# Folding a weight by halves, reading V in long rows that are transposed twice, and a second PSUM pair for attention values

## Chip, cores, metric

One core of one Trainium2 chip. The metric is the device time of one execution in microseconds (us); lower is better. All times compared below are of the state called fast; slow executions (over 1.5% above the fastest of the same kernel) are left out of the ratios, with one exception: run e12 has an execution of 313.05 us that is listed as slow, and its ratio comes out only with that execution counted in (see "The clock"). The quoted medians are over all executions.

## The reference

```python
def _attn_ref(q, k, v):                    # 8 batches, 8 heads, 576 rows, 64 columns
    scores = (1 / np.sqrt(64)) * np.matmul(q, k.transpose(0, 1, 3, 2))
    rel = pos[:, None] - pos[None, :]
    scores = np.where((rel >= 0) & (rel < 64), scores, -1e9)      # window of 64, causal
    attn = softmax(scores)
    return np.matmul(attn, v)

x = attn_out.transpose(0, 2, 1, 3).reshape(4608, 512)
out = ((x @ w1) * (x @ w2) @ w3) @ w_out   # w1, w2: 512x1024, w3: 1024x1024, w_out: 1024x512
```

## The kernel before

`w3 @ w_out` is folded once, on the chip, into `wc_sb`; after that, the feed-forward of a group of 512 rows is `ffn_ab` (eight times) and `ffn_o` (four times). Attention runs as `scores`, an exponential on ScalarE, masks on GpSimd, and `values`. The first two batches are a hand-ordered prologue; from the third on a loop interleaves attention of one batch with the feed-forward of another.

In these traces an engine takes its own instructions in program order. So where a line stands in this code decides what its copies stand behind. PSUM in the text is the memory that these kernels' matmuls write to (tiles f_ps, s_ps, o_ps and tp in the profile's lines) and that other engines then copy out of.

```python
def load_v(b, *blocks):                # V straight into key blocks, short rows, GpSimd queue
    ...
        nc.gpsimd.dma_start(out=vh[lo:P, c], in_=v[b, :, s0:s0 + P - lo, :].rearrange("h s d -> s h d"))
def copy_v(b, c):                      # rows that two key blocks share
    vh = v_heads(b)
    dve_cp(vh[0:D, c], vh[D:P, c - 1])
    if c == 1:
        dve_cp(vh[D:P, 1], vh[0:D, 2])
def fold_t(fc):                        # turn one block of w3
    ...
    dve_cp(w3T, tp)
def fold_mm(fc, w3T, cp):              # multiply it by the whole of w_out
    for ec in range(8):
        nc.tensor.matmul(o_ps, w3T[:, ec, :], wo16[:, ec, :], start=(ec == 0), stop=(ec == 7))
    cp(wc_sb[:, fc, :], o_ps)
def fold_step(fc):                     # the turn runs one block ahead of the fold
    if fc + 1 < 8:
        w3Ts[fc + 1] = fold_t(fc + 1)
    fold_mm(fc, w3Ts.pop(fc), act_cp if fc % 4 == 3 else dve_cp)
# ... cut: the prologue's first stretch
for d in range(5):
    ...
    values(d)
    if d < 4:
        scores(d + 2)
    fold_step(d + 2)
    # ... cut: loads of batch 1, its k casts on VectorE and ScalarE, its q casts on GpSimd and ScalarE
```

## Time and profile before

| | before |
|---|---|
| time, median of 3 (range) | 296.19 us (295.75 to 296.27) |
| profiled span | 294.3 us |
| first turn of w3 (the fold starts) | 19.71 us |
| first feed-forward matmul | 46.85 us |
| start of the repeating part | 81.27 us |

A timeline line gives start, length, engine, line of the kernel, operation, what it writes and reads, shapes, and in brackets the idle time just before with the engine or transfer that ended it. The readings of before, with their lines, are in the prediction. The stretches A (fold start to first feed-forward matmul), B (to the repeating part) and C (the rest) are used in the same sense throughout.

### The profile page before, as it was taken

Reading aid. Unit: us, or ns where it says so; the run is one execution under the profiler, and the core shown is the slowest. Engines: PE = TensorE matmul, PEld = TensorE weight load, DVE = VectorE, ACT = ScalarE, POOL = GpSimd, SP = SyncE. Lnnn points to the kernel's source line nnn. Section 1 sums busy time; section 2 is a strip of 40 time slices with the busy share of each in tenths; the row PEclk is TensorE's granted clock in tenths of the full one; section 3 lists DMA queues with packets and bytes.
Section 4 is the critical chain, followed back from the end, with each engine's and each line's share of the span. In section 5 each row is a group of like instructions: output and inputs, shape, how many; then the busy total and the mean of one; then the engine's idle time right before and its main releaser. Section 6 shows DMA issues by size and latency. Waiting matters only on the chain.

```text
span 294.3 us, 5925 instructions
## 1 busy us (share of the span) xinstructions
PE 274.1 (93%) x2254; PEld 152.9 (52%) x2254; DVE 185.4 (63%) x289; ACT 168.4 (57%) x281; POOL 180.8 (61%) x214
## 2 busy tenths in 40 slices
PE   7758889898799999999999999999999999999992
PEld 7544555444455555555555787555555445444440
DVE  0715688465787667687777866677867555554541
ACT  2513774676458647766686565487568866642300
POOL 8835995478749856696869463786595344402200
PEclk9999999999999999999999999999999999999998
DMA  6999999990277939094929470950094021012012
GB/s 231 219 181 201 265 278 212 373 131 36 74 266 264 72 110 321 39 85 143 322 20 100 136 295 2 155 73 1 20 171 40 0 74 72 0 38 109 0 57 95
DMA packets 51665, 38.85 MB, mean 132 GB/s; under 512 B 38784, under 2 KB 41856, under 8 KB 51632
## 3 DMA queue, kind: packets, MB, share of 16 engines
q0 software_dynamic: 41744, 9.96, 36.2%
q1 hardware_dynamic: 9888, 28.46, 26.6%
q8 instruction: 19, 0.31, 0.4%
q14 instruction: 14, 0.11, 0.1%
HBM read 38.80 MB, written 9.44 MB: 164 GB/s over the span
## 4 chain that ended last, share of the span: by engine, by line
PE 76%; DVE 6%; ACT 5%; DMA 4%; issue 3%; POOL 3%; POOLq 0%; DVEq 0%; ACTq 0%
PE f_ps L395 38%; PE f_ps L408 19%; PE o_ps L311 7%; PE tp L253 5%; DMA ab<-in_moe_w_dram 4%; PE s_ps L278 4%; DVE xT L327 2%; PE f_ps L454 2%; ACT ln_s L321 2%; ACT r L323 2%; POOL v L488 2%; DVE kT L257 1%; DVE xT L326 1%; ACT ln_s L320 1%; ACT pt L282 1%
## 5 line engine op out<-in xcount | busy, mean ns | idle before, releaser
L395 PE MATMUL f_ps<-xT,w_sb 128*128 128x512 f16 (+1 forms) x640 | 134.1, 358 | 0.0
L290 POOL TENSOR_SCALAR_AFFINE_SELECT pt<-pt 128x512 f16<-128x512 f16 (+1 forms) x64 | 52.1, 814 | 69.0 <-ACT pt L282 68.9
L395 PEld LDWEIGHTS <-w_sb 128*128 128x128 f16 x640 | 59.7, 98 | 50.7 <-issue 0.5
L408 PE MATMUL f_ps<-wc_sb,ab 128*128 128x512 f16 x288 | 67.1, 379 | 0.1
L401 DVE TENSOR_TENSOR ab<-f_ps,a_sb 128x512 f16<-128x512 f32 x72 | 49.8, 692 | 18.4 <-PE f_ps L395 15.8
L326 DVE TENSOR_TENSOR xT<-o_ps,r 64x384 f16<-64x384 f32 x48 | 26.4, 550 | 53.8 <-ACT r L323 53.6
L282 ACT ACTIVATE pt<-s_ps 128x1024 f16<-128x1024 f32 (+1 forms) x48 | 45.5, 949 | 18.0 <-PE s_ps L278 16.5
L400 ACT COPY a_sb<-f_ps 128x512 f32<-128x512 f32 x72 | 41.7, 579 | 24.8 <-PE f_ps L395 23.9
L292 POOL TENSOR_SCALAR_AFFINE_SELECT pt<-pt 128x512 f16<-128x512 f16 (+1 forms) x64 | 52.4, 819 | 4.4
L320 ACT ACTIVATE ln_s<-o_ps 64x384 f32<-64x384 f32 x48 | 23.4, 487 | 53.4 <-PE o_ps L311 53.3
L408 PEld LDWEIGHTS <-ab 128*128 128x128 f16 x288 | 26.9, 98 | 28.8 <-DVE ab L401 0.6
L233 POOL DMA_DIRECT2D v<-in_v_dram x40 | 33.9, 854 | 5.9 <-DMA ab<-in_moe_w_out_dram 4.1
L311 PE MATMUL o_ps<-pt,v 128*128 128x128 f16 (+1 forms) x384 | 27.9, 215 | 5.9 <-DVE xT L327 4.0
L311 PEld LDWEIGHTS <-v 128*128 128x128 f16 x384 | 23.5, 98 | 18.2 <-issue 3.5
L410 DVE COPY t2k<-f_ps 128x512 f32<-128x512 f32 x36 | 24.7, 690 | 11.6 <-PE f_ps L408 11.1
L327 DVE TENSOR_TENSOR xT<-o_ps,r 64x384 f16<-64x384 f32 x48 | 26.9, 561 | 0.6
L323 ACT ACTIVATE r<-ln_s 128x384 f32<-128x384 f32 x48 | 25.1, 523 | 1.5
L321 ACT ACTIVATE ln_s<-o_ps 64x384 f32<-64x384 f32 x48 | 23.1, 482 | 0.5
L278 PEld LDWEIGHTS <-kT 64*128 64x128 f16 x384 | 10.5, 94 | 16.5 <-issue 14.8
L278 PE MATMUL s_ps<-qT,kT 64*128 64x128 f16 (+1 forms) x384 | 18.2, 214 | 0.3 <-ACT pt L282 0.2
L257 DVE COPY kT<-tp 128x768 f16<-128x768 f16 x17 | 16.2, 952 | 0.1
L454 PE MATMUL f_ps<-ab,t2k 128*128 128x512 f16 x64 | 15.0, 379 | 0.4 <-DVE t2k L448 0.3
(59 smaller groups left out, 179.8 us busy)
## 6 DMA issues: line engine op xcount, KB each, us to landing
stage<-in_k_dram SPq DMA_DIRECT2D x16, 576.0 KB
stage<-in_q_dram SPq DMA_DIRECT2D x16, 576.0 KB
out_dram<-t2k SPq DMA_DIRECT2D x36, 256.0 KB
v<-in_v_dram POOLq DMA_DIRECT2D x32, 128.0 KB, 4.7
w_sb<-in_moe_w_dram POOLq DMA_DIRECT2D x4, 512.0 KB, 9.5
ab<-in_moe_w_out_dram POOLq DMA_DIRECT2D x1, 1024.0 KB, 10.6
ab<-in_moe_w_dram POOLq DMA_DIRECT2D x2, 512.0 KB, 12.6
xT<-in_moe_w_dram POOLq DMA_DIRECT2D x2, 512.0 KB, 16.2
```

The lines of the kernel that those rows point to most:

```text
L233: nc.gpsimd.dma_start(out=vh[lo:P, c], in_=v[b, :, s0:s0 + P - lo, :].rearrange("h s d -> s h d"))
L278: nc.tensor.matmul(s_ps[:, a, jj, c0:c0 + n], kT[half, j, k0:k0 + P], qT[half, j, q0:q0 + n], start=True, stop=True, skip_group_check=True)
L282: nc.scalar.activation(pt[:, :, :, 0:w], s_ps[:, :, :, 0:w], AF.Exp, bias=-SHIFT, scale=scale)
L290: nc.gpsimd.affine_select(out=sl, in_=sl, pattern=pat, compare_op=ALU.is_ge, fill=0.0, base=off, channel_multiplier=-1)
L292: nc.gpsimd.affine_select(out=sl, in_=sl, pattern=[[-s, m] for s, m in pat], compare_op=ALU.is_ge, fill=0.0, base=63 - off, channel_multip ...
L311: nc.tensor.matmul(o_ps[:, jj, o0:o0 + n], v16[:, si * 2 + bi, j0 + jj, a * D:a * D + P], pt[:, a, jj, c0:c0 + n], start=first, stop=(bi = ...
L323: nc.scalar.activation(r, y, AF.Exp, scale=-1.0)
L327: nc.vector.tensor_tensor(xs[D:P], o_ps[D:P, :, 192:384], r[D:P], ALU.mult)
L395: nc.tensor.matmul(d[:, f * n + c0:f * n + c1], w[:, dc, (fc + f) * P:(fc + f + 1) * P], xT[:, dc, xc:xc + c1 - c0], start=first, stop=(dc ...
L400: act_cp(a_sb[:, 0:nf * n], a_ps[:, 0:nf * n])
L401: nc.vector.tensor_tensor(ab[:, fc:fc + nf, lo:hi], b_ps[:, 0:nf * n].rearrange("p (f n) -> p f n", f=nf), a_sb[:, 0:nf * n].rearrange("p ...
L408: nc.tensor.matmul(o_ps, ab[:, fc, t * P:t * P + P], wc_sb[:, fc, :], start=(fc == 0), stop=(fc == 7))
```

## The change

Its intent: start the fold sooner by waiting for half of w_out; let the scores of batch 0 run before its V is there; read V of batches 0 and 1 with few large packets and put it in place by two rounds of transposes on TensorE; give the values two PSUM pairs in turn so that they need not wait for each other. w3 is turned in place. The core of the diff:

```diff
+    def load_rows(b, which):              # long rows, cast to fp16 by the transfer
+        t = sb.tile([P, 2, TI * D], FP16, name="rows")
+        for hh in range(2):
+            nc.gpsimd.dma_start(out=t[:, hh], in_=big_rows(which, b, hh))
+    def keys_of_v(b, js, into, cps):      # second transpose of V, into key blocks
+        for j, tp in zip(js, into):
+            for c in range(6):
+                nc.tensor.transpose(tp[:, c, :], turned["v", b][:, j, VBLK[c]:VBLK[c] + P], ident16)
+        ...
-        o_ps = ps_v.tile([P, 2, 512], FP32, name="o_ps")
+        o_ps = ps_v.tile([P, 2, 512], FP32, name="o_ps") if pool is None else \
+            ps_s.tile([P, 2, 512], FP32, name="s_ps")
-    def load_wo():
+    def load_wo(half):
-    def fold_mm(fc, w3T, cp):
+    def fold_mm(fc, half, cp, nf=1):
...
+    fold_t(0)
+    scores(2)
+    load_rows(1, "k")
+    fold_mm(0, 0, dve_cp)
+    fold_t(1)
+    scores(3)
+    fold_mm(1, 0, dve_cp)
...                                        # cut: the same for 2 and 3
+    cast_qk(0, "v", 0, dve_cp)
+    cast_qk(0, "v", 1, act_cp)
+    load_rows(1, "q")
+    transposes(0, "v", 0, 1, 2, into=spare(ps_v, "o_ps") + [tp_bank()], cps=[dve_cp, act_cp, dve_cp])
+    fold_t(4, act_cp)
+    fold_mm(4, 0, dve_cp)
+    keys_of_v(0, [0, 1, 2, 3], spare(ps_v, "o_ps") + spare(ps_s, "s_ps"), [dve_cp, act_cp, dve_cp, act_cp])
+    fold_t(5)
+    values(0)
+    fold_mm(5, 0, dve_cp)
+    fold_t(6)
+    values(1, ps_s)
+    fold_mm(6, 0, dve_cp)
...
+    for d in range(3, 6):
+        fold_mm(2 * d - 6, 1, dve_cp, 2)   # second half of w_out, two blocks at a time
+        values(d, ps_s if d % 2 else None)
+    fold_mm(6, 1, dve_cp, 2)
+    for hh in range(2):
+        cast_qk(1, "k", hh, dve_cp)
+    load_rows(1, "v")
+    for i in range(2):
+        load_w12(i, 1)
+    ffn_ab(0, 0)
+    transposes(1, "k", 0, 1, 2, into=spare(ps_s, "s_ps") + [tp_bank()])
+    ffn_ab(0, 1)
+    for hh in range(2):
+        cast_qk(1, "q", hh, dve_cp)
...
+    transposes(1, "q", 0, 1, 2, into=spare(ps_v, "o_ps") + [tp_bank()])
+    ffn_ab(0, 2)
+    scores(6)
+    cast_qk(1, "v", 0, dve_cp)
+    cast_qk(1, "v", 1, act_cp)
+    transposes(1, "v", 0, 1, 2, into=spare(ps_v, "o_ps") + [tp_bank()], cps=[dve_cp, act_cp, dve_cp])
```

More of the change, by code (lines that the diff above doesn't have):

```diff
@@ L195, with big_rows @@
     v16s = [const.tile([P, 6, NJ, 4 * D], FP16, name=f"v16_{i}") for i in range(2)]
-    raws, k16s, q16s = {}, {}, {}
+    raws, t16s = {}, {}
+    def big_rows(which, b, hh):
+        return {"k": k, "q": q, "v": v}[which][b, hh:H:2].rearrange("j (p r) d -> p j (r d)", r=TI)
     def load_qk(b, which, gate=None):
-        src = k if which == "k" else q
-        t = sb.tile([P, 2, TI * D], FP32, name="stage", bufs=4)
+        t = sb.tile([P, 2, TI * D], FP32, name="stage", bufs=3)
         if gate is not None:
@@ L205, in load_qk, with t16_of @@
         for hh in range(2):
-            nc.sync.dma_start(out=t[:, hh], in_=src[b, hh:H:2].rearrange("j (p r) d -> p j (r d)", r=TI))
+            nc.sync.dma_start(out=t[:, hh], in_=big_rows(which, b, hh))
         raws[which, b] = t
-    def cast_qk(b, which, hh, cp):
-        t = raws[which, b]
-        if hh == 0:
-            (k16s if which == "k" else q16s)[b] = sb.tile([P, TI, P], FP16, name=which + "16", bufs=1)
-        t16 = (k16s if which == "k" else q16s)[b]
-        cp(t16[:, :, hh * D:hh * D + D], t[:, hh].rearrange("p (i d) -> p i d", d=D))
-    def cast_third(b, which, c, cp):
-        t = raws[which, b]
-        if c == 0:
-            (k16s if which == "k" else q16s)[b] = sb.tile([P, TI, P], FP16, name=which + "16", bufs=1)
-        t16 = (k16s if which == "k" else q16s)[b]
-        cp(t16[:, 6 * c:6 * c + 6].rearrange("p i (hh d) -> p hh i d", hh=2),
-           t[:, :, 6 * c * D:6 * c * D + 6 * D].rearrange("p hh (i d) -> p hh i d", d=D))
+    def load_rows(b, which):
+        t = sb.tile([P, 2, TI * D], FP16, name="rows")
+        for hh in range(2):
+            nc.gpsimd.dma_start(out=t[:, hh], in_=big_rows(which, b, hh))
+        raws[which, b] = t
+    def t16_of(b, which):
+        if (which, b) not in t16s:
+            t16s[which, b] = sb.tile([P, TI, P], FP16, name=which.replace("v", "k") + "16", bufs=1)
+        return t16s[which, b]
+    def cast_qk(b, which, hh, cp):
+        cp(t16_of(b, which)[:, :, hh * D:hh * D + D], raws[which, b][:, hh].rearrange("p (i d) -> p i d", d=D))
+    def cast_third(b, which, c, cp):
+        cp(t16_of(b, which)[:, 6 * c:6 * c + 6].rearrange("p i (hh d) -> p hh i d", hh=2),
+           raws[which, b][:, :, 6 * c * D:6 * c * D + 6 * D].rearrange("p hh (i d) -> p hh i d", d=D))
     def v_heads(b):
@@ L239, in copy_v @@
             dve_cp(vh[D:P, 1], vh[0:D, 2])
-    kTs, qTs = {}, {}
+    turned = {}
     def transposes(b, which, *cs, into=None, cps=None):
-        t16, dst = (k16s, kTs) if which == "k" else (q16s, qTs)
+        t16 = t16s[which, b]
         if cs[0] == 0:
-            dst[b] = sb.tile([P, NJ, S], FP16, name=which + "T")
+            turned[which, b] = sb.tile([P, NJ, S], FP16, name=which + "T", bufs=1 if which == "v" else 2)
+        dst = turned[which, b]
         if into is None:
@@ L252, in transposes @@
             for i in range(6):
-                nc.tensor.transpose(tp[:, i, :], t16[b][:, 6 * c + i, :], ident16)
+                nc.tensor.transpose(tp[:, i, :], t16[:, 6 * c + i, :], ident16)
         if cps is None:
@@ L256, in transposes @@
         for c, tp, cp in zip(cs, into, cps):
-            cp(dst[b].rearrange("q j (p i) -> q j p i", i=TI)[:, :, :, 6 * c:6 * c + 6],
+            cp(dst.rearrange("q j (p i) -> q j p i", i=TI)[:, :, :, 6 * c:6 * c + 6],
                tp.rearrange("q i (p j) -> q j p i", p=TP))
+    def keys_of_v(b, js, into, cps):
+        for j, tp in zip(js, into):
+            for c in range(6):
+                nc.tensor.transpose(tp[:, c, :], turned["v", b][:, j, VBLK[c]:VBLK[c] + P], ident16)
+        for j, tp, cp in zip(js, into, cps):
+            cp(v16s[b % 2][:, :, j].rearrange("p c (a e) -> p c a e", a=2)[:, :, :, 0:D],
+               tp.rearrange("p c (a e) -> p c a e", a=2))
     MASKS = [[(0, 1, 128, 0, 0), (128, 1, 64, 64, 0)]] + 2 * [[(0, 2, 128, 64, -64)]]
@@ L267, in scores @@
         si, jp = divmod(r, 2)
-        kT, qT = kTs[b], qTs[b]
+        kT, qT = turned["k", b], turned["q", b]
         seg = SEGS[si]
@@ L280, in scores @@
                 c0 += n
-        pt = sb.tile([P, 2, 2, 256], FP16, name="pt", bufs=3)
+        pt = sb.tile([P, 2, 2, 256], FP16, name="pt", bufs=6)
         nc.scalar.activation(pt[:, :, :, 0:w], s_ps[:, :, :, 0:w], AF.Exp, bias=-SHIFT, scale=scale)
@@ L294, in scores, with values @@
         probs[d] = pt
-    def values(d):
+    def values(d, pool=None):
         b, r = divmod(d, 6)
@@ L430, in load_w12 @@
                             in_=(moe_w1, moe_w2)[i][:, cols].rearrange("(c p) n -> p c n", p=P))
-    def load_wo():
-        nc.gpsimd.dma_start(out=wo16, in_=moe_w_out.rearrange("(e p) m -> p e m", p=P))
+    def load_wo(half):
+        cols = slice(half * 256, half * 256 + 256)
+        nc.gpsimd.dma_start(out=wo16[:, :, cols], in_=moe_w_out[:, cols].rearrange("(e p) m -> p e m", p=P))
     def load_w3(n):
@@ L439, in load_w3, with turned_w3, fold_t @@
         nc.gpsimd.dma_start(out=dst, in_=moe_w3[fc * P:fc * P + 2 * P].rearrange("(f p) n -> p f n", p=P))
-    def fold_t(fc):
-        w3 = w3_rows(fc).rearrange("p a (e n) -> p (a e) n", n=P)
+    def turned_w3(fc):
+        return w3_rows(fc).rearrange("p a (e n) -> p (a e) n", n=P)
+    def fold_t(fc, cp=dve_cp):
+        w3 = turned_w3(fc)
         tp = ps_f.tile([P, 8, P], FP16, name="f_ps")
@@ L446, in fold_t @@
             nc.tensor.transpose(tp[:, ec, :], w3[:, ec, :], ident16)
-        w3T = sb.tile([P, 8, P], FP16, name="t2k", bufs=4)
-        dve_cp(w3T, tp)
-        return w3T
-    def fold_mm(fc, w3T, cp):
-        o_ps = ps_f.tile([P, DM], FP32, name="f_ps")
-        for ec in range(8):
-            nc.tensor.matmul(o_ps, w3T[:, ec, :], wo16[:, ec, :], start=(ec == 0), stop=(ec == 7))
-        cp(wc_sb[:, fc, :], o_ps)
+        cp(w3, tp)
+    def fold_mm(fc, half, cp, nf=1):
+        cols = slice(half * 256, half * 256 + 256)
+        o_ps = ps_f.tile([P, 2, 256], FP32, name="f_ps")
+        for f in range(nf):
+            for ec in range(8):
+                nc.tensor.matmul(o_ps[:, f], turned_w3(fc + f)[:, ec, :], wo16[:, ec, cols],
+                                 start=(ec == 0), stop=(ec == 7), skip_group_check=True)
+        cp(wc_sb[:, fc:fc + nf, cols], o_ps[:, 0:nf])
     rows = 2 * 3 * B
@@ L491 @@
     ones_of(1)
-    load_wo()
+    load_wo(0)
     load_w3(0)
-    load_v(0, 0, 2, 3)
-    for n in range(1, 4):
-        load_w3(n)
-    load_v(0, 4, 5)
-    w3Ts = {}
-    def fold_step(fc):
-        if fc + 1 < 8:
-            w3Ts[fc + 1] = fold_t(fc + 1)
-        fold_mm(fc, w3Ts.pop(fc), act_cp if fc % 4 == 3 else dve_cp)
+    load_w3(1)
+    load_rows(0, "v")
+    load_w3(2)
+    load_w3(3)
+    load_wo(1)
     def spare(pool, name):
@@ L509, in spare, with tp_bank @@
         return [t[:, i, 0:768].rearrange("p (i n) -> p i n", i=6) for i in range(2)]
+    def tp_bank():
+        return ps_t.tile([P, 6, P], FP16, name="tp")
     keep_busy(75)
@@ L518 @@
         cast_third(0, "q", c, act_cp if c == 1 else dve_cp)
-    tps = [tps[3], ps_t.tile([P, 6, P], FP16, name="tp"), spare(ps_s, "s_ps")[0]]
-    transposes(0, "q", 0, 1, 2, into=tps, cps=[act_cp, dve_cp, act_cp])
+    transposes(0, "q", 0, 1, 2, into=[tps[3], tp_bank(), spare(ps_s, "s_ps")[0]], cps=[act_cp, dve_cp, act_cp])
     keep_busy(15)
     scores(0)
-    keep_busy(10)
+    keep_busy(12)
     scores(1)
-    keep_busy(30)
     for i in range(2):
         load_w12(i, 0)
-    w3Ts[0] = fold_t(0)
@@ L529 @@
-    fold_step(0)
-    fold_mm(1, w3Ts.pop(1), dve_cp)
-    copy_v(0, 1)
-    for d in range(5):
-        if d == 0:
-            w3Ts[2] = fold_t(2)
-        values(d)
-        if d < 4:
-            scores(d + 2)
-        fold_step(d + 2)
-        if d == 0:
-            load_v(1, 0, 2)
-            load_qk(1, "k", nc.vector.memset)
-            load_qk(1, "q")
-        if d == 1:
-            load_v(1, 3)
-        if d == 2:
-            copy_v(0, 4)
-            for i in range(2):
-                load_w12(i, 1)
-        if d == 3:
-            load_v(1, 4)
-            cast_qk(1, "k", 0, dve_cp)
@@ L552 @@
-    cast_qk(1, "k", 1, act_cp)
-    cast_qk(1, "q", 0, pool_cp)
-    cast_qk(1, "q", 1, act_cp)
-    values(5)
-    fold_step(7)
-    transposes(1, "k", 0, 1, into=spare(ps_s, "s_ps"))
-    transposes(1, "k", 2)
+    keep_busy(12)
+    fold_t(0)
[5 more added lines that the diff above has]
+    fold_mm(1, 0, dve_cp)
+    fold_t(2)
+    scores(4)
+    fold_mm(2, 0, act_cp)
+    fold_t(3)
+    scores(5)
+    fold_mm(3, 0, dve_cp)
+    cast_qk(0, "v", 0, dve_cp)
@@ new lines @@
+    cast_qk(0, "v", 1, act_cp)
[10 more added lines that the diff above has]
+    fold_mm(6, 0, dve_cp)
+    fold_t(7)
+    values(2)
+    fold_mm(7, 0, dve_cp)
+    for d in range(3, 6):
+        fold_mm(2 * d - 6, 1, dve_cp, 2)
+        values(d, ps_s if d % 2 else None)
@@ L559 @@
+    fold_mm(6, 1, dve_cp, 2)
[4 more added lines that the diff above has]
+        load_w12(i, 1)
     for n in range(3):
         keep_sums(n)
-    load_v(1, 5)
+    ffn_ab(0, 0)
[3 more added lines that the diff above has]
+        cast_qk(1, "q", hh, dve_cp)
     load_qk(2, "k", nc.gpsimd.memset)
     load_qk(2, "q")
-    load_v(2, 0, 2, 3)
-    ffn_ab(0, 0)
@@ L566 @@
-    transposes(1, "q", 0, 1, into=spare(ps_s, "s_ps"))
-    transposes(1, "q", 2)
-    copy_v(1, 1)
-    ffn_ab(0, 1)
+    transposes(1, "q", 0, 1, 2, into=spare(ps_v, "o_ps") + [tp_bank()])
     ffn_ab(0, 2)
     scores(6)
+    cast_qk(1, "v", 0, dve_cp)
+    cast_qk(1, "v", 1, act_cp)
+    load_v(2, 0, 2, 3)
+    transposes(1, "v", 0, 1, 2, into=spare(ps_v, "o_ps") + [tp_bank()], cps=[dve_cp, act_cp, dve_cp])
     ffn_ab(0, 3)
     scores(7)
-    steps = [lambda fc=fc: ffn_ab(0, fc) for fc in range(4, 8)] + [lambda t=t: ffn_o(0, t) for t in range(3)]
@@ L577 @@
-    for d in range(6, 11):
-        values(d)
-        if d < 10:
-            scores(d + 2)
-        for _ in range(2 if d in (6, 8) else 1):
-            steps.pop(0)()
-            store()
+    keys_of_v(1, [0, 1, 2], spare(ps_v, "o_ps") + [tp_bank()], [dve_cp, act_cp, dve_cp])
+    scores(8)
+    keys_of_v(1, [3], [tp_bank()], [dve_cp])
+    steps = [lambda fc=fc: ffn_ab(0, fc) for fc in range(4, 8)] + [lambda t=t: ffn_o(0, t) for t in range(4)]
+    for d in range(6, 12):
+        values(d, ps_s if d in (9, 11) else None)
+        if d < 9:
+            scores(d + 3)
+        steps.pop(0)()
+        store()
@@ L584 @@
         if d == 6:
             load_v(2, 4, 5)
-            copy_v(1, 4)
             load_qk(3, "k")
-        else:
-            which, hh = [("k", 0), ("k", 1), ("q", 0), ("q", 1)][d - 7]
-            cast_qk(2, which, hh, pool_cp)
-    transposes(2, "k", 0, 1, into=spare(ps_s, "s_ps"))
-    values(11)
+        if d < 10:
+            cast_qk(2, "kq"[(d - 6) // 2], d % 2, pool_cp)
+    transposes(2, "k", 0, 1, into=spare(ps_v, "o_ps"))
     transposes(2, "k", 2)
@@ L595 @@
         cast_qk(3, "k", hh, pool_cp)
-    ffn_o(0, 3)
+    steps.pop(0)()
     store()
@@ L599 @@
     transposes(2, "q", 2)
+    load_qk(3, "q")
+    steps.pop(0)()
+    store()
     copy_v(2, 1)
     copy_v(2, 4)
-    load_qk(3, "q")
     for n in range(3, 6):
```

## The prediction

> **What bounds the kernel now.** I first read the busy shares by slice on the profile's page: the TensorE row is at 9 from the eleventh of 40 slices to the last but one, and uneven before that.
>
> ```profile
> PE   7758889898799999999999999999999999999992
> DMA  6999999990277939094929470950094021012012
> ```
>
> So what is open to a gain lies in the first quarter. The chain of work that ended last gave me where to cut it: the weight fold starts at 19.71 us, when the first rows of w3 land; the feed-forward starts at 46.85; and at 81.27 the prologue is over and the repeating part begins, whose code the diff does not touch. A table of busy time in these three stretches (length, then TensorE matmul, weight load, VectorE, ScalarE, GpSimd, then clock, DMA share, GB/s):
>
> ```profile
> 19.71:46.85 27.14, 24.09 (x227) 13.86 (x228) 17.59 (x31) 15.87 (x26) 23.59 (x30) 1.00 1.39 237
> 46.85:81.27 34.42, 30.14 (x249) 16.02 (x247) 22.75 (x36) 19.28 (x33) 22.50 (x26) 1.00 0.77 160
> 81.27:294.30 213.03, 206.67 (x1594) 111.06 (x1590) 139.37 (x217) 126.35 (x214) 121.43 (x142) 0.99 0.47 106
> ```
>
> TensorE is idle 27.14 - 24.09 = 3.1 us in the first stretch (call it A), 4.3 us in the second (B). In C it is 97% busy, so whatever moves the start of C moves the end. The waits themselves, from the timeline of TensorE alone (start, length, what, and in brackets idle time before and who ended it):
>
> ```profile
> 19.71 1.07 PE L446 MATMUL f_ps<-ident,ab 128*128 128x128 f16 x16 [2.71 <-DMA ab<-in_moe_w_dram]
> ...
> 36.58 0.61 PE L311 MATMUL o_ps<-pt,v 128*128 128x128 f16 x8 [0.27 <-DVE xT L327]
> 37.12 0.40 PE L278 MATMUL s_ps<-qT,kT 64*128 64x128 f16 x8
> 37.45 0.62 PE L446 MATMUL f_ps<-ident,xT 128*128 128x128 f16 x8
> 37.91 1.89 PE L454 MATMUL f_ps<-ab,t2k 128*128 128x512 f16 x8
> 39.97 0.62 PE L311 MATMUL o_ps<-pt,v 128*128 128x128 f16 x8 [0.18 <-DVE xT L327]
> ```
>
> One round of A (values, scores, turn of w3, fold) lasts 3.4 us. The chain of o (two logarithms of 0.49, a reciprocal of 0.53, two multiplications of 0.56 us, then the next values) lasts just as long, so the single PSUM pair for o costs only 0.2 to 0.3 us a round. The lines by shape give the unit costs (count, busy us, mean ns of one, idle before):
>
> ```profile
> L257 DVE COPY kT<-tp 128x768 f16<-128x768 f16 x17 | 16.2, 952 | 0.1
> L257 ACT COPY qT<-tp 128x768 f16<-128x768 f16 x5 | 4.0, 808 | 0.0
> L448 DVE COPY t2k<-f_ps 128x1024 f16<-128x1024 f16 x8 | 5.4, 691 | 7.9 <-PE f_ps L446 7.7
> L214 ACT CAST k<-stage 128x1152 f16<-128x1152 f32 x1 | 1.1, 1136 | 0.0
> L214 DVE CAST k<-stage 128x1152 f16<-128x1152 f32 x1 | 0.8, 845 | 0.0
> ```
>
> [...]the 32 matmuls that cross the ring's end (two cuts for 512 columns, so 256 on average) took 3.49 us, 109 ns each, against 3.45 us for 16 of 512. So halves cost TensorE nothing. [...]here 768 fp16 elements out of PSUM take 0.95 us and 512 within SBUF (the V copies) 0.29. [...]in the windows of 1 us the casting queue writes 200 to 210 GB/s with weights alone and 155 to 160 while V blocks are among them. [...]the loss is small.
>
> **The change part by part.**
>
> *Start of the fold.* Before it 1.05 MB of w_out and 0.52 MB of w3 have to land (written bytes). Half of w_out is now enough: 0.52 MB less at 200 GB/s is 2.6 us; with the V blocks no longer close behind, 3.3. The 12 dummy matmuls left after the second scores end near 16.0, so the fold starts at about 16.4: 3.3 us gained. V, the rest of w3, the other half and w1, w2 land by about 36 at 205 GB/s, ahead of their use.
>
> *Work added to TensorE.* Each of two batches gets 18 + 24 transposes for V. Six in a stream move the chain by 0.34 us[...], so 84 cost 4.8 us. Nothing is removed from it but 16 dummy matmuls that only filled a wait.
>
> *The upper limit.* 3.3 earlier + 3.1 + 4.3 of idle time, less 4.8 of new work: 5.9 us, if no wait were left. That is just 2%.
>
> *Waits in A, set down engine by engine in program order from the fold's start (0).* A round of scores, turn and half fold is 0.45 + 0.33 + 0.86 of TensorE, but fold follows the turn of the same rows: turn, copy 0.69, then fold, and the copy also stands behind the last fold's eviction (about 0.38). Such a round is 2.3 us with 0.6 idle; four end at 9.1. The casts of V stand behind the last eviction on VectorE and the last exp on ScalarE, so V's first transposes start at 10.4 (1.3 idle) and end at 11.4. Fold 4 waits for ScalarE's copy of 1024 columns until 13.1; the second transposes end at 15.4, their copies at 16.5. Values 0, 1, 2 go in at 16.0, 18.5, 21.7: the copy of each turn stands behind the multiplications of the values before on VectorE, so the folds wait 0.7 to 1.4 us each. Then the four double folds and three values run dense until 31.9, and the feed-forward waits for the last multiplication: 33.0. Of these 33 us TensorE works 23.8. A thus ends at 16.4 + 33 = 49.4, against 46.85, and the 18 transposes of k, which stood in A, are still to come.
>
> *Waits in B, from its start (0).* Casts and copies that GpSimd and ScalarE shared are on VectorE. Transposes of q wait for two casts (about 0.6 each, fp16 source; an estimate from 0.29 for 512 elements) that stand behind three 0.95 copies of k and one product: start 7.5, TensorE idle since 4.7, 2.8 us. Transposes of V wait for a cast on ScalarE of 1.1 behind the exp: 2.2 us. The fourth group of V's second transposes waits for its PSUM bank to be copied: 1.1. Values 7 and 8 wait for o, 0.8 each, as now; smaller ones sum to some 2.5. TensorE's work is 28.4 (now, by starts) + 1.0 (k) + 2.4 (V) = 31.8; with about 10 of waits, 42. VectorE has some 34 us of work in it, against 22.75. C starts at 49.4 + 42 = 91.4, against 81.3.
>
> The sum is +10 us. I don't take it whole: a worked list counts every wait in full, and a wait of 0.3 to 0.5 put wrong in each of twenty places is 6 to 10 us, more likely too much than too little, since I rounded starts upward. I take some 70%: +7, so 303.
>
> **The rivals.** *The earlier fold wins through:* the copies and casts fall into gaps, the two PSUM pairs remove the waits for o, and C starts 1 to 4 us earlier: 292 to 295. For it: VectorE is busy only 65% in A and 66% in B, and all its new work there is under the length. Against it: [...]the new copies stand between turn and fold. *DMA is the true limit:* shares above 1 in A and V's 36,864 small packets of 41,744 suggest a gain through A and B from long rows. Against it: TensorE's only long wait for DMA is the 2.7 us at the start; V's 9,216 packets less free nothing on the path. It would give 291 to 294. *A new transfer wait:* rows of V of batch 1 and the second halves of w1 and w2 are now issued on GpSimd only after a cast at the end of A, so they land near 60, needed at 61 and 69; two us late would add two: 305 to 308. *The repeating part suffers* from three input buffers in place of four; by the order of loads and casts each slot is free before it is wanted, so nothing.
>
> **Range and chances.** 303, range 293.5 to 309.5: the low end is the first rival, the high end the full sum and a late transfer. Faster by over 2% needs more than the limit above: 3%. Within 2% (up to 302.1) holds the first two rivals and the lower part of my sum: 39%. Slower: 58%.
>
> **What would show it.** Right: fold's first turn near 16.4; first feed-forward matmul near 49; waits of TensorE before the folds for VectorE's copies of the turned w3, and before the transposes of q and V for casts; start of C near 88 to 91; C as long as now, 213. Wrong: C starting before 82, or the fold's rounds below 2.0 us, or C shorter by 3 us or more, which no step here explains.

## The result

The changed kernel took 309.97 us (median of four, 308.72 to 311.48) against 296.18 (median of four): ratio 1.047, 95% interval 1.042 to 1.052. Ratios in this text are the mean time of one kernel's fast runs over that of the other's fast runs of the same rounds, so not quite the ratio of the quoted medians; those of the experiments come out, as far as they can be redone from the listed times, only if the profiled execution is left out. The kernel got slower, as held likeliest, but by 13.8 us where 6.8 was predicted, and just outside the range.

The table by stretch of the kernel after; columns as in the prediction (length, TensorE matmul, weight load, VectorE, ScalarE, GpSimd, then clock, DMA share, GB/s):

```profile
16.18:50.51 34.33, 26.86 (x314) 23.43 (x315) 18.92 (x32) 17.77 (x28) 15.32 (x21) 0.95 0.77 135
50.51:95.61 45.10, 36.81 (x309) 20.63 (x307) 29.84 (x46) 22.55 (x37) 26.28 (x32) 0.92 0.70 146
95.61:308.20 212.59, 206.65 (x1591) 111.03 (x1589) 138.90 (x216) 125.83 (x214) 121.47 (x142) 1.00 0.48 107
```

The fold starts 3.5 us earlier (16.18 against 19.71). A is 7.2 us longer, B 10.7 us longer, C the same within 0.5 us. The repeating part starts at 95.61 instead of 81.27: 14.3 us later, which is the whole loss. The third column from the right is the one whose change the prediction had no step for: the mean granted TensorE clock is 0.95 in A and 0.92 in B, where it was 1.00 in both before.

The waits of TensorE in A and B, longest groups first (what it was about to do, what it waited for: sum, times, longest), kernel after:

```profile
PE f_ps L477 <- DVE xT L469: 2.3, 3, 1.8
PE o_ps L261 <- DVE q L225: 2.1, 1, 2.1
PE f_ps L477 <- ACT xT L469: 2.0, 1, 2.0
PE o_ps L261 <- ACT k L225: 2.0, 1, 2.0
PE f_ps L477 <- DVE ab L469: 1.8, 4, 0.5
PE o_ps L329 <- DVE xT L345: 1.3, 2, 0.7
```

L477 is the fold, L469 the copy of the turned w3, L261 the transposes of q, k and V, L225 a cast (V uses the name of k). So these are the waits that the prediction set down: folds for the copy that they follow at once, transposes for their casts. On TensorE's timeline, with what came after each (kernel after):

```profile
16.18 0.62 PE L468 MATMUL f_ps<-ident,ab 128*128 128x128 f16 x8 [0.23 <-DMA ab<-in_moe_w_dram]
...
30.39 1.05 PE L477 MATMUL f_ps<-ab,xT 128*128 128x256 f16 x8 [2.02 <-ACT xT L469]
...
54.31 1.89 PE L413 MATMUL f_ps<-xT,w_sb 128*128 128x512 f16 x8
...
58.26 0.93 PE L261 MATMUL o_ps<-ident,q 128*128 128x128 f16 x12 [2.05 <-DVE q L225]
...
59.61 3.22 PE L413 MATMUL f_ps<-xT,w_sb 128*128 128x512 f16 x8
...
65.12 0.95 PE L261 MATMUL o_ps<-ident,k 128*128 128x128 f16 x12 [2.01 <-ACT k L225]
...
66.50 3.19 PE L413 MATMUL f_ps<-xT,w_sb 128*128 128x512 f16 x8
```

The group of eight feed-forward matmuls at 54.31 takes 1.89 us, as before. The same group takes 3.22 us shortly after the wait at 58.26 and 3.19 us after the one at 65.12. Windows of one microsecond show the reason, the third number from the right being the granted clock:

```profile
32.00:33.00 1.00, 1.00 (x12) 1.00 (x10) 0.50 (x1) 0.00 (x0) 0.00 (x0) 0.50 1.27 219
60.00:61.00 1.00, 1.00 (x4) 0.41 (x3) 1.00 (x2) 0.79 (x1) 0.00 (x0) 0.50 1.20 260
```

After each of the three waits of 2.0 us the clock is at half for 3.4 us (a dip, below): 0.50, where it is 1.00 around it. The dips start at 31.58, 58.88 and 65.71 us (by windows of 0.1 us), and each lasts 3.41 us. The second and third start 8.0 and 10.0 times 3.41 us after the first, so in this trace they lie on a grid of 3.41 us; a step of the grid, counted from a dip of the same run, is called a window in what follows. The windows just before the three dips hold 2.02, 2.05 and 2.01 us of idle TensorE time. The length of a wait alone does not tell what follows it: after the wait of 2.71 us in the kernel before the clock is 1.00.

In the two runs set side by side here it goes with where in a window a wait falls. The profiled execution of e12 (below; only the issue of two transfers is moved) has the same three waits, of 2.02, 2.05 and 2.01 us, and a single dip, from which its windows are counted back. Two windows of the kernel after, the one with the wait before q's transposes and the next, then the windows of e12 with its second wait (two windows) and its third, and the next (TensorE's busy time is the second number):

```profile
55.47:58.88 3.41, 1.36 (x15) 0.75 (x14) 2.73 (x5) 0.49 (x1) 0.73 (x2) 1.00 1.00 180
58.88:62.30 3.42, 3.42 (x17) 1.77 (x15) 1.82 (x2) 1.40 (x2) 0.00 (x0) 0.50 1.17 265
```

```profile
53.14:56.55 3.41, 2.07 (x15) 0.87 (x12) 3.36 (x5) 0.59 (x1) 0.60 (x2) 1.00 0.79 121
56.55:59.97 3.42, 2.70 (x26) 1.70 (x26) 2.48 (x4) 0.83 (x2) 0.00 (x0) 1.00 1.03 323
59.97:63.38 3.41, 1.40 (x26) 1.13 (x26) 1.10 (x3) 2.31 (x3) 1.81 (x4) 1.00 1.03 416
63.38:66.79 3.41, 3.41 (x13) 1.23 (x10) 1.78 (x2) 1.40 (x2) 2.86 (x4) 0.50 1.19 373
```

The wait of 2.05 us is cut in two by the end of a window (1.34 and 0.72 us idle), and the clock stays at 1.00; the one of 2.01 us lies inside a window, and the next is at 0.50. No clean limit comes out of the runs, though. In e12 a fourth wait, of 2.20 us up to 38.03, lies with 1.95 us in one window by the same count, and the folds after it take their usual 1.05 us. In e1 (below) the window from 37.86 to 41.27, counted on from its dip at 27.62, has 2.03 us idle, and the groups after it are as fast as ever (0.61 and 1.05 us). In e11, against that, two waits of 0.96 and 0.72 us between 57.7 and 60.3 us are followed by a group of 3.23 us in place of 1.90. So idle time within a window is not all that counts, and what else does was not shown. The number of dips may then differ between executions of one kernel, and the times fit that: e12's four executions take 307.30, 308.69, 311.39 and 313.05 us at mean clocks of 0.989, 0.984, 0.973 and 0.967.

Last, the GpSimd queue. It stood for 21.55 us before the DMA issue of the rows of V of batch 1, which waited for a cast on VectorE, with the second halves of w1 and w2 behind them, and the transfer engines were almost idle from 38 to 54 us (the DMA row has one digit per 7.7 us slice; digits six and seven fall there):

```profile
53.53 1.07 POOL L216 DMA_DIRECT2D rows<-in_v_dram  x2 [21.55 <-DVE k L225]
```

```profile
DMA  6999900999416993829483954092049003003012
```

### The profile page after: what moved, and what is told of

Read it like the earlier page. It is cut to its first block, busy times and chain, and to the rows that moved or that the text cites. A ratio compares the mean times of both kernels' runs of the same rounds, so it can differ in the third digit from the quotient of the medians.

```text
span 308.2 us, 6193 instructions
## 1 busy us (share of the span) xinstructions
PE 282.2 (92%) x2386; PEld 165.9 (54%) x2386; DVE 193.1 (63%) x300; ACT 173.1 (56%) x286; POOL 176.1 (57%) x212
## 4 chain that ended last, share of the span: by engine, by line
PE 76%; DVE 9%; ACT 5%; DMA 4%; issue 2%; POOL 2%; POOLq 0%; ACTq 0%; DVEq 0%
PE f_ps L413 36%; PE f_ps L426 20%; PE o_ps L329 5%; PE tp L261 5%; PE s_ps L295 4%; PE f_ps L477 3%; DMA ab<-in_moe_w_dram 3%; POOL v L512 2%; DVE xT L345 2%; DVE kT L265 2%; DMA stage<-in_k_dram 1%; ACT ln_s L339 1%; ACT r L341 1%; DVE xT L344 1%; ACT pt L299 1%
## 5 line engine op out<-in xcount | busy, mean ns | idle before, releaser
L413 PE MATMUL f_ps<-xT,w_sb 128*128 128x512 f16 (+1 forms) x640 | 137.1, 363 | 0.6 <-DVE xT L345 0.6
L413 PEld LDWEIGHTS <-w_sb 128*128 128x128 f16 x640 | 60.6, 99 | 53.0 <-issue 4.5
L344 DVE TENSOR_TENSOR xT<-o_ps,r 64x384 f16<-64x384 f32 x43 | 23.6, 550 | 47.3 <-ACT r L341 47.3
L338 ACT ACTIVATE ln_s<-o_ps 64x384 f32<-64x384 f32 x43 | 20.9, 487 | 36.8 <-PE o_ps L329 36.1
L329 PE MATMUL o_ps<-pt,v 128*128 128x128 f16 x344 | 24.9, 216 | 1.7 <-DVE xT L345 1.7
L240 POOL DMA_DIRECT2D v<-in_v_dram x30 | 25.4, 854 | 0.0
L345 DVE TENSOR_TENSOR xT<-o_ps,r 64x384 f16<-64x384 f32 x43 | 24.1, 561 | 0.6
L339 ACT ACTIVATE ln_s<-o_ps 64x384 f32<-64x384 f32 x43 | 20.7, 482 | 0.5
L225 POOL CAST k<-stage 128x1152 f16<-128x1152 f32 x12 | 13.8, 1151 | 2.0 <-PE tp L261 2.0
```

What stands on the lines that cost most here:

```text
L329: nc.tensor.matmul(o_ps[:, jj, o0:o0 + n], v16[:, si * 2 + bi, j0 + jj, a * D:a * D + P], pt[:, a, jj, c0:c0 + n], start=first, stop=(bi = ...
L344: nc.vector.tensor_tensor(xs[0:D], o_ps[0:D, :, 0:192], r[0:D], ALU.mult)
L345: nc.vector.tensor_tensor(xs[D:P], o_ps[D:P, :, 192:384], r[D:P], ALU.mult)
L413: nc.tensor.matmul(d[:, f * n + c0:f * n + c1], w[:, dc, (fc + f) * P:(fc + f + 1) * P], xT[:, dc, xc:xc + c1 - c0], start=first, stop=(dc ...
```

## The experiments

Theory: the loss is the sum of waits that the new program order makes (turn directly before its fold; casts before transposes), in full and not at 70%, plus lost clock after the longest. Rivals: the transfers issued late are the limit; or one part alone (the transposes of V) carries the loss. The runs undo parts of the change, or fill waits without removing them.

| run | what was altered | ratio to before (95%) |
|---|---|---|
| the change | | 1.047 (1.042 to 1.052) |
| e1_fill_waits | three waits filled with dummies | 1.042 (1.039 to 1.044) |
| e8_fill_all | five waits filled | 1.040 (1.036 to 1.044) |
| e9_fill_all_w12_early | five filled, w1 and w2 issued sooner | 1.033 (1.030 to 1.036) |
| e12_w12_early | only w1 and w2 issued sooner | 1.048 (1.043 to 1.054) |
| e2_q_cast_gpsimd | q casts off VectorE | 1.034 (1.029 to 1.040) |
| e3_turn_ahead | turn one block ahead of fold | 1.025 (1.021 to 1.029) |
| e4_v_blocks | V as before | 1.025 (1.020 to 1.030) |
| e6_one_pair | one PSUM pair for the values | 1.062 (1.058 to 1.066) |
| e7_whole_w_out | whole w_out first | 1.053 (1.045 to 1.061) |
| e5_three_undone | e2, e3 and e4 | 1.009 (1.006 to 1.012) |
| e10_three_undone_w12_early | e5, w1 and w2 sooner | 1.008 (1.003 to 1.012) |
| e11_rebuilt | all rewritten, halves and pairs kept | 1.012 (1.007 to 1.016) |
| e13_order_of_before | e10 up to the feed-forward, then before's code | 0.999 (0.995 to 1.003) |
| e14_v_copy_scalar | e13, three copies of V on ScalarE | 0.993 (0.990 to 0.996) |
| e15_v1_before_q_cast | e14, first V blocks of batch 1 sooner | 0.991 (0.987 to 0.995) |

All outputs are right. The line numbers of the experiments' profiles differ by a few from those of the kernel after.

### The clock

The change's own profile has three dips. e1 puts 28 dummy matmuls, some 1.7 us, into each of three waits; nothing can start sooner for it.

```diff
     fold_t(4, act_cp)
+    fill(28)
     fold_mm(4, 0, dve_cp)
...
+    fill(28)
     transposes(1, "q", ...
...
+    fill(28)
     transposes(1, "v", ...
```

> 28 dummy matmuls (1.7 us at 0.062 each) are put into three waits of TensorE of 2.0 us each (before the fold of rows 4, before the transposes of q and of V of batch 1). In the changed kernel the granted clock falls to 0.50 for some 3.3 us after each of these waits. Theory (part of the loss is the clock): no stretch at 0.50 is left between 28 and 70 us, the feed-forward group at 59.6 takes 1.9 us in place of 3.2 and the one at 66.5 too, the repeating part starts 3 to 4.5 us earlier, 305.5 to 307 us. Rival (the waits alone, the clock is made good elsewhere): within 1 us of 310.

Measured: 308.91 us, 1.6 less than after in the ratio's terms (0.0054 of 296); the profiled execution, 306.87, is the fastest of the four and alone inside the expected range. The timeline of TensorE in e1:

```profile
56.91 1.73 PE L509 MATMUL f_ps<-ident 128*128 128x128 f16 x28
59.12 0.84 PE L261 MATMUL o_ps<-ident,q 128*128 128x128 f16 x12 [0.49 <-DVE q L225]
59.80 0.50 PE L261 MATMUL tp<-ident,q 128*128 128x128 f16 x6
60.14 1.89 PE L413 MATMUL f_ps<-xT,w_sb 128*128 128x512 f16 x8
```

TensorE gets to its transposes no sooner after the group before them than without dummies, but the group after them is back at 1.89 us from 3.22. So here idle TensorE time, not the work itself, brought the half clock. The time fell by less than expected: the dip at 31 to 35 us was only replaced by one at 27.6 to 31.0 (0.50 in windows of one microsecond), after a wait of 1.68 us that I had not filled, and a wait of 0.5 us for w1 or w2 appeared. e8 fills two more waits.

```diff
+    fill(18)
     transposes(0, "v", ...
...
+    fill(24)
     fold_mm(6, 0, dve_cp)
```

> As the first filler run, and also 18 dummies before the transposes of V of batch 0 (wait 1.3 us) and 24 before the fold of rows 6 (wait 1.8 to 2.2). Theory (the granted clock is part of the loss): no stretch under 0.9 of the full clock between 20 and 75 us, 2.5 to 4.5 us less than the changed kernel, 305.5 to 307.5, and less spread from run to run. Rival (a low clock costs nothing, since TensorE waits anyway): 308.5 to 310.

Measured 309.15 us (2.2 below after by the ratio): a miss. The list of TensorE's waits in e8 starts with:

```profile
PE f_ps L413 <- DMA w_sb<-in_moe_w_dram: 2.9, 1, 2.9
```

TensorE is now at a point where the late halves of w1 and w2 are needed, and waits for them 2.9 us; the four matmuls behind that wait (74.15) take 1.89 us where the four before it took 1.04, and the next two groups are slow as well (0.85 for 0.51, 0.61 for 0.40), until 77.15: the half clock again, as an estimate from these lengths. e9 issues them earlier, ahead of the rows of V that hold up the queue; e12 does this alone.

```diff
     load_rows(1, "q")
+    for i in range(2):
+        load_w12(i, 1)
...
-    for i in range(2):
-        load_w12(i, 1)
```

> As the run with all waits filled, and the second halves of w1 and w2 are issued on GpSimd before the rows of V of batch 1 (which wait there for the casts of k) and not behind them. Theory (filling the waits gained only 1 us because the feed-forward then ran into these weights, a wait of 2.9 us on DMA, which the changed kernel hid behind its own lateness): that wait goes, 305.5 to 307.5. Rival (the clock is worth no more than 1 us): 308.5 to 310.

> The changed kernel with only the earlier issue of the second halves of w1 and w2, a control. Theory (there the weights land some 4 us ahead of use, since TensorE is late): 309 to 311, no change. Rival (the issue order itself costs the changed kernel time): under 308.

Measured: e9 306.69 us, e12 310.04. Both as expected. e12's ratio of 1.048 counts the slow execution of 313.05 us; without it 310.04 us, or 1.045, is left (from two executions, so a rough figure). e9 is then 3.6 us below its control e12 by the ratio, 3.3 by medians, and 4.3 below the change itself by the ratios of the table. Windows of 4 us show a clock of 1.00 throughout from 20 to 92 us in e9. The late transfer is not on the path of the changed kernel (e12 does not differ from it within the noise) but is the next limit behind the clock (e8). The lost clock is worth 3.3 to 4.3 us.

### The program order

e3 lets each turn run one block ahead. It also casts V one fold earlier and moves the copy of the fifth turn from ScalarE to VectorE (not shown):

```diff
     fold_t(0)
     scores(2)
-    fold_mm(0, 0, dve_cp)
     fold_t(1)
+    fold_mm(0, 0, dve_cp)
     scores(3)
-    fold_mm(1, 0, dve_cp)
     fold_t(2)
+    fold_mm(1, 0, dve_cp)
...
```

> The turn of each w3 block stands one block ahead of its fold, as in the kernel before; all else as changed. Theory: the four waits of 0.46, the 2.0 before the fold of rows 4, and the 1.8, 0.3 and 0.2 further on go (6.2 us in all), and the low clock after the second one (about 1.6 us); some of it comes back as waits for the casts of V: 4 to 7 us less, 303 to 306. Rival (w3's arrival or the logarithms of o bound this stretch): under 2 us less.

Measured 304.32 us: 6.6 us by the ratio. The feed-forward starts at 45.51 instead of 50.51. The four waits of the folds for VectorE's copy, 1.8 us in all, and the one of 2.0 us for ScalarE's are gone from the list. The three edits were not separated.

e2 moves the q casts of batch 1 from VectorE, behind three copies of 0.95 us, to GpSimd, right after `fold_mm(7, 0, ...)`:

```diff
     fold_mm(7, 0, dve_cp)
+    for hh in range(2):
+        cast_qk(1, "q", hh, pool_cp)
...
-    for hh in range(2):
-        cast_qk(1, "q", hh, dve_cp)
```

> The two casts of q of batch 1 go from VectorE to GpSimd, which is idle for 21 us there, and before the end of the fold. Theory (waits behind VectorE's order, and the clock after them): the wait of 2.05 us before the transposes of q goes, and with it the low clock after it (1.3 us): 306 to 307. Without the clock's part: 308. Rival (another releaser stands behind the same wait, for instance the copies of k): no change, 309.5 to 310.

Measured 307.44 us, 3.8 us by the ratio (2.5 by medians): the wait of 2.05 us is gone, and the dip of the clock behind it (the group there takes 1.89 us again).

### V

e4 loads V of batches 0 and 1 in blocks with `copy_v`, and has no casts and transposes of V.

```diff
-    load_rows(0, "v")
+    load_v(0, 0, 2, 3)
...
-    cast_qk(0, "v", 0, dve_cp)
-    cast_qk(0, "v", 1, act_cp)
-    transposes(0, "v", ...)
+    copy_v(0, 1)
+    copy_v(0, 4)
...
-    keys_of_v(0, [0, 1, 2, 3], ...)
```

(the same for batch 1)

> V of batches 0 and 1 comes in blocks in its final layout again, without casts and transposes; fold by halves, scores ahead and two PSUM pairs stay. Theory (V's long rows cost most of the loss): 84 transposes (4.8 us), the waits for their casts (1.3 and 2.0), for the copy on ScalarE (2.0) and for the bank (0.45) and the low clock after two of them (2.9) go: 10 to 13 us less, 297 to 300. Rival (V's small packets now delay w3 or V itself, which long rows had cured): the fold starts over 1 us later or waits for DMA show, over 302. Rival (the loss lies in the fold's halves and order): over 304.

Measured 304.73 us, 6.5 us by the ratio: a miss, the rival's number came. 84 transposes, four casts and their waits are gone, but new waits stand in their place. Three lines of e4's waits of TensorE:

```profile
PE f_ps L477 <- DVE xT L469: 4.0, 2, 2.4
PE o_ps L329 <- POOL pt L309: 1.8, 3, 0.6
PE s_ps L329 <- POOL pt L309: 1.0, 1, 1.0
```

Values wait for their masks on GpSimd, and folds for VectorE's copies of the turned w3, 2.4 us at the longest. Just ahead of that copy VectorE ran the three copies of `copy_v` for 1.02, 1.12 and 2.15 us while GpSimd was at masks (from 28 to 32 us VectorE is busy for 3.94 us and GpSimd for 3.93); e13 and e14 below take up what held them. A dip follows that wait too, from 32.0 to 35.5 us (clock 0.57 in the window from 32 to 36).

e5 joins e2, e3 and e4; e10 adds the earlier w1 and w2.

> The three edits that each helped (turn of w3 one ahead, q casts on GpSimd early, V of batches 0 and 1 in blocks) together; fold by halves, scores ahead and two pairs for o stay. Theory (the loss is in the waits and work of these three parts): the single gains were 6.5, 3.8 and 6.1 us; the wait before the fold of rows 4 is counted in two of them, so some 14 in sum: 294 to 298, the time before. Rival (the gains cover one another, a further bound lies behind them, such as GpSimd's mask work in the fold): 299 to 303.

> As the run with the three parts undone together, with the same earlier issue. Theory (its wait of 3.4 us on DMA for w1 and w2 hid part of the three gains): 295.5 to 297. Rival (masks on GpSimd or transfers bind in another place): 298 to 300.

Measured 299.36 and 298.47 us, ratios 1.009 and 1.008: of the 13.9 us lost, some 11 come back together, less than 6.6 + 3.8 + 6.5. That the parts share waits is one likely reason; it was not tested. In e5 TensorE waited 3.4 us for w1 and w2; with these early, e10 waits for masks in their place, and the ratio moves by no more than its interval. Both missed what I had expected, and the rivals' numbers came.

### The parts that were good

e6 gives all values one PSUM pair (`values(1, ps_s)` becomes `values(1)`, and so on). e7 loads the second half of w_out right behind the first.

> All outputs o go through one PSUM pair, as before the change; all else as changed. Theory: each of the later values of batch 0 stands 0.3 to 1 us behind the multiplications of the one before, but the double folds are there to fill, so 0 to 2 us more: 310 to 312. Rival (the second pair itself costs, since it makes values wait for scores): less than 309.

> Both halves of w_out are read ahead of w3, as before the change; the fold's order stays. Theory (the early start is real and is kept to the end, since the stretch after it is a chain of waits): first turn at about 19, 2.5 to 3 us more, 312 to 313. Rival (the fold's start was hidden, V's rows or w1 and w2 bound its end): 310 to 311.

e6: 315.81 us, 4.3 us above after by the ratio (5.8 by medians), more than expected. Its first wait of TensorE:

```profile
PE o_ps L329 <- DVE xT L345: 7.8, 7, 1.6
```

In the kernel after, that line reads 1.3 us in two waits. The second pair was worth 0.2 to 0.3 us a round in the old order; in the new one it is worth much more, probably because values follow each other faster there. e7: 313.01 us, with the first turn of w3 at 18.78 us. The median is what was expected, but the interval of its ratio (1.045 to 1.061) overlaps that of the change (1.042 to 1.052), so the loss is not told apart from noise.

### What is left of it when rearranged

e11 rewrites both stretches: V in blocks, k and q loaded as before, half folds with the turn ahead, two PSUM pairs. e13 is e10 up to the last fold (with the casts of k and the k transposes of before behind it), and the code of before from the first `ffn_ab` on.

> A version meant to beat both: fold by halves with the early start, turn one block ahead, scores ahead and two pairs for o are kept; V comes in blocks, k and q of batch 1 by the sync queue with casts spread over three engines, and transfers are issued on GpSimd so that no wait stands ahead of weights. By the same working as in the prediction (fold from 16.5, some 23 us of TensorE work to the feed-forward, o's chain and GpSimd's masks beside it, then some 36 us): 288 to 292. If transfers bind (14.3 MB read ahead of the feed-forward at some 380 GB/s is 38 us, and its w1 and w2 come in between): 293 to 297.

> The fold stretch as in the run with three parts undone and early weights (feed-forward ready from 42.9), and from the first feed-forward on the kernel before's order: V of batch 2 loaded early, two steps in two of the rounds, masks two pairs ahead, k transposed before the feed-forward. Theory (what is left of the loss, 1.25 us, is the changed order after the fold, where GpSimd's masks stand behind casts and V loads: that stretch took 39.6 against 34.4 + 1.0): the repeating part starts at 78 to 80, 293 to 295.5, under the kernel before. Rival (the earlier feed-forward only meets a transfer or a mask sooner, so the gain of the early fold is eaten): 296.5 to 299.

The kernel before moved 376 to 390 GB/s from 35 to 40 us (windows of one microsecond); the 380 in what was expected of e11 is of that size.

e11: 300.27 us, a clear miss (288 to 292 expected); TensorE waited 3.4 us for VectorE's copies of the turned w3, 2.3 for a copy of V and 1.7 for exponentials. e11's median holds one slow execution (302.60). e13: 296.93 us, level with before; the rival's number. Its repeating part starts at 81.25 (before 81.27), though the fold starts at 17.77 and there are two PSUM pairs. TensorE's one long wait in its fold stretch, and what VectorE and GpSimd did then (kernel e13; VectorE first):

```profile
30.39 0.46 PE L329 MATMUL o_ps<-pt,v 128*128 128x64 f16 x7 [3.00 <-DVE v L246]
```

```profile
26.93 1.22 DVE L244 COPY v<-v 64x512 f16<-64x512 f16 x1
28.18 2.15 DVE L246 COPY v<-v 64x512 f16<-64x512 f16 x1
```

```profile
26.91 1.10 POOL L309 TENSOR_SCALAR_AFFINE_SELECT pt<-pt 128x1024 f16<-128x1024 f16 x1
27.95 1.11 POOL L216 DMA_DIRECT2D rows<-in_k_dram  x2
29.05 1.13 POOL L307 TENSOR_SCALAR_AFFINE_SELECT pt<-pt 128x1024 f16<-128x1024 f16 x1
30.25 1.10 POOL L309 TENSOR_SCALAR_AFFINE_SELECT pt<-pt 128x1024 f16<-128x1024 f16 x1
```

Copies of this form take 0.29 us in the median of the kernel before (both lines, 24 of them). Here the first ends at 28.15, 0.14 after the mask at 26.91 ended; the second ends at 30.33, 0.15 after the mask at 29.05 ended, and its 2.15 us span the rest of a DMA issue (27.95 to 29.06) and then the whole mask. The kernel before has the same: its copies at 131.14, 158.84 and 193.73 take 1.68, 1.68 and 1.24 us and end 0.15 to 0.16 us after a mask, and those at 52.18, 83.13 and 105.77, with GpSimd idle, take 0.28 to 0.29. So these copies seem to stand behind GpSimd's instructions: 1.22 and 2.15 us in place of 0.29, with ends tied to GpSimd's; a DMA issue need not stretch them (0.29 us at 26.04 and 62.51 in the kernel before, each inside one). e14 tests it by moving these copies, for batch 0 only:

```diff
-        dve_cp(vh[0:D, c], vh[D:P, c - 1])
+        cp = act_cp if b == 0 else dve_cp
+        cp(vh[0:D, c], vh[D:P, c - 1])
         if c == 1:
-            dve_cp(vh[D:P, 1], vh[0:D, 2])
+            cp(vh[D:P, 1], vh[0:D, 2])
```

> The kernel of e13_order_of_before with one thing changed: the three copies per batch 0 that put V's shared rows in place are on ScalarE instead of VectorE. In e13 TensorE waited 3.0 us for the second of these copies, which took 2.15 us on VectorE (the first 1.22) although the same form takes 0.29 when GpSimd is idle; GpSimd then was in masks and a DMA issue without a gap from 25.7 to 33.4 us. If VectorE's copy within SBUF stood behind GpSimd's instructions, ScalarE's copies are not stretched (each below 0.8 us), the wait falls to 1.2 us or less, the clock stays at 1.00 from 31 to 34 us (it fell to 0.50 in e13, which cost about 1.5), and the time is 293 to 295.5. Rival: the copies wait for V or for the write of both halves whatever the engine, or another wait (masks for the values, 1 us each) ends only as late: 296 to 298.

Measured 293.82 us, ratio 0.993 (0.990 to 0.996), inside the expected range. In e14's timeline the copies on ScalarE and the first values of TensorE are:

```profile
24.58 0.62 ACT L245 COPY v<-v 64x512 f16<-64x512 f16 x1
25.22 0.62 ACT L247 COPY v<-v 64x512 f16<-64x512 f16 x1
```

```profile
27.97 0.50 PE L330 MATMUL o_ps<-pt,v 128*128 128x128 f16 x8
```

The values no longer wait, the clock is 1.00 from 27 to 35 us, and the feed-forward starts at 42.53 instead of 45.80 (0.6 of it from a fold that started sooner in this run). On ScalarE the copies take 0.62 us each (the third, at 30.07, too, in a microsecond that GpSimd is busy throughout). So they were held up on VectorE and not by a late V. They also start 1.8 us sooner after the fold's start than in e13, since ScalarE reaches them sooner; but two copies of 0.29 us from 26.93 would have ended at 27.5 (an estimate), so the stretching alone makes up most of e13's wait of 3.00. By whole times the gain of e14 over e13 is 2 to 3 us (ratio, medians), and the two intervals overlap slightly (0.990 to 0.996 and 0.995 to 1.003). Of the 3.3 us by which the feed-forward starts sooner, 2.1 arrive at the repeating part (79.16); a wait of 1.80 us in B, where a product on VectorE stands behind copies of V of batch 1 whose transfer is late, is one place where the rest goes. e15 issues those blocks before the q casts on GpSimd:

```diff
+    load_v(1, 0, 2)
     for hh in range(2):
         cast_qk(1, "q", hh, pool_cp)
-    load_v(1, 0, 2, 3, 4, 5)
+    load_v(1, 3, 4, 5)
```

> The kernel of e14_v_copy_scalar with one thing changed: blocks 0 and 2 of V of batch 1 are issued on GpSimd before its two casts of q, not after. In e14 GpSimd stood idle for 1.79 us before those casts, then issued V 2.4 us later, and in the second stretch VectorE waited 1.3 and 1.0 us for these blocks with a product of the feed-forward behind the copies, for which TensorE waited 1.80 us. If that is all, the two waits for the transfer and TensorE's 1.80 fall away: 291.8 to 293. Rival: the q casts come later by the issues (0.8 us each) and TensorE waits for q's transposes instead, or the masks are next: 293 to 295.

Measured 294.17 us (292.37 to 296.12), ratio 0.991 (0.987 to 0.995): not told apart from e14. In the profiled run, one of the two longest at 296.0 us, the wait is still there at 2.5 us, and the group after it takes 3.47 us, where 1.89 is usual, as at the half clock. What e15 was to decide stays open. e14 and e15 beat both kernels, before by 0.7 to 0.9%.

## Why the prediction was right or wrong

*Fold start: right.* 16.18 measured for 16.4. With the whole of w_out first (e7) the fold starts at 18.78, 2.6 us later, and the time is 1.7 (ratio) to 3.0 us (medians) longer. That the earlier start reaches the end is likely but not shown, since the intervals overlap.

*The upper limit: not tested.* No version came near 5.9 us; the best, without V's transposes, gained 2 to 3.

*Waits in A: right.* 34.33 us measured for 33.0, which the half clock at 31 to 35 us accounts for: 3.4 us at half speed cost some 1.5 (an estimate). The four waits of 0.46 us before folds (0.6 foreseen), the one for ScalarE's copy (2.02; about 1.25 foreseen) and the one before V's transposes (1.3 both) are there by name. The 1.1 us foreseen before the feed-forward came only in B, as 0.60, so part of the agreement is two errors of 0.8 and 1.1 us that cancel. In e3, with the turn ahead, the waits before the folds are gone.

*Waits in B: nearly right.* 45.10 us for 42. The wait for q's casts was 2.05 (2.8 foreseen), that for V's cast 2.01 (2.2), that for the bank 0.4 (1.1), those for o 1.3 in sum (1.6). The two slow groups cost 1.33 and 1.30 us, 2.6 of the 3.1, and the slowed transposes ahead of them some 0.7 more. VectorE's work in B was put too high (29.84 us for 34).

*"I don't take it whole ... I take some 70%: +7": wrong.* This is one of two steps that failed. The full sum gave 91.4 for the start of C; without the clock's share (estimated above, 1.5 + 2.6 us) the trace gives 91.5, or 90.8 without the slowed transposes too. The sum did not count too much. The reason given for the discount, that starts had been rounded upward, was not checked against any line, and it cost 3 us. The sum is better than its parts, though. TensorE's idle time was 7.5 us in A and 8.3 in B, where 9.2 and some 10 were foreseen, and its work without the clock's share (an estimate) was some 25.4 and 33.5, where 23.8 and 31.8 were: the waits were 3.4 us too long, the work 3.3 too short. Part of that is the way of counting (work taken from start to start makes a wait begin earlier), the rest is luck; the record does not separate them. So a discount on the waits was not absurd, but it was put on the whole sum.

*No step for the clock: the other failure.* The prediction's tables for before showed 1.00 beside a wait of 2.71 us, and I took the clock as constant. e9 against e12 and the change shows 3.3 to 4.3 us. With both, 303 becomes 303 + 3 + 4 = 310; 309.97 was measured. That it fits so closely is luck in part, since the number of dips may differ from one execution to the next.

*C: right.* 212.59 against 213.03, so three input buffers cost nothing that can be seen. (One reading of the page is off by a slice: TensorE's row is at 9 throughout from the twelfth of 40 slices on, the eleventh has a 7. Nothing rests on it. And the 0.95 us of a copy out of PSUM, which the prediction sets beside 0.29 within SBUF, is not the price of PSUM alone: copies of the same 128x768 out of PSUM took 0.56 us into V's key blocks in the kernel after, where the layouts differ.)

*The rivals.* The earlier fold does not win through, though one part of that rival, the second PSUM pair, is worth more than I said: 4 to 6 us in this order (e6), against 0.2 to 0.3 a round in the old. DMA as the limit: wrong for this kernel: V in blocks again is 6.5 us faster (e4). The late transfer: not on the path (e12), but hidden close behind it (e8, e5).

*What stays open.* Undoing three parts leaves 0.8% (e10). With the code of before in the second stretch it is gone (e13), but the two intervals nearly touch (1.003 to 1.012 and 0.995 to 1.003), and which of the waits for masks, exponentials and products mattered was not separated. Why the wait of 2.71 us in the kernel before left the clock at 1.00 is not settled either: it may have been cut by the end of a window as in e12, but the only dip of that trace starts at 291.5 us, after the last matmul, too far off to count windows back from.

## What to carry to other kernels

When waits have been worked out engine by engine in program order, do not discount their sum unless a line of the profile contradicts it; and leave room for the clock, read from the clock column. Here each dip of 3.41 us at 0.50 cost dense work some 1.7 us (an estimate from these two numbers), and of three waits of 2.0 us all brought one in the kernel after and one did in e12. Keep something between producing and using (the turn one block ahead of its fold, with V's casts moved too, was worth 6.6 us), and look for what stands behind a blocked transfer in the same queue (here w1 and w2, behind one of 21.55 us). Where GpSimd is busy, look at the length of short VectorE copies within SBUF on the path: here three of them, 0.82 to 2.15 us long in e13 for 0.29 in the median of the kernel before, were better on ScalarE at 0.62 (e14).
